# Decode attention with its key and value loads regrouped into four units of 32 KB rows, and its feed-forward part moved to the front

## The chip, the cores and the metric

The kernel runs on one core of a Trainium2 chip. The metric is the time of one execution in microseconds on the device. Executions of the same kernel differ, so each is called fast or slow: slow is a run more than 1.5 % above the fastest of the same kernel. The profile gives the span of the profiled execution, first to last instruction. The time is about 1.8 us longer than the span.

## The reference

Batch 2, one new token, 16 query heads on 8 key/value heads of size 256, a window of 2048 cached positions, and a small feed-forward part (FFN below) whose result gates the attention output.

```python
xn = layernorm(x)                                  # x: (2, 1, 448)
q  = xn @ wq                                       # 448 x 4096
s  = softmax(q @ K[window].T * 256**-0.5) @ V[window]
s  = s @ wo                                        # 4096 x 448
g  = silu(relu(xn @ w1) @ w2)                      # 448 x 1792, 1792 x 448
return x + s * g
```

K and V of the window are 33.6 MB of the 44.1 MB that the kernel reads. Each byte is used once, so the stream of loads is the floor: at the about 420 GB/s of the profile below, 44.1 MB take 105 us.

## The kernel before

K and V come as 16 transfers each of 1 MB, one per pair of head and batch, with 8 KB contiguous per partition. There are six K buffers and eight V buffers. One queue, that of the SP engine, issues all loads in order; a load waits until the buffer that it overwrites has been read.

```python
NT = W // 128; NKB = 6; NVB = 8
def kv_src(c, cache):                 # one head, one batch: 128 partitions x 8 KB
    hkv, b = divmod(c, 2)
    return cache[b, hkv, SK - W:SK, :].rearrange("(p t) d -> p (t d)", t=NT)
def load_k(c):
    d_k[c] = pr.dma(SP, kbuf[c % NKB][:, :], kv_src(c, A_k_cache), [last_T.get(c - NKB)])
def load_v(c):
    d_v[c] = pr.dma(SP, vbuf[c % NVB][:, :], kv_src(c, A_v_cache), [last_PV.get(c - NVB)])

load_k(0); load_k(1)
d_wq = pr.dma(SP, wqo[:, 0:SLOTS * HC], wq_src)
load_k(2); load_k(3)
# ... K and V alternate, V one pair behind K; and at the end of the program:
load_w1(0); load_w2(0)
# ... wo in five pieces, then on PE:
do_H(0); do_H(1); do_hT(); ...; do_F()          # the FFN
# ... 128 output matmuls with wo, gate, add x, store
```

PE transposes each K chunk (four 128x128 transposes, "T"), DVE or ACT copies the result from PSUM to SBUF (an eviction), PE multiplies by q (scores, "S"), softmax follows on DVE, PE and ACT, and PE multiplies the transposed weights by V ("PV").

Of the kernel before, what the change touches and what calls it, by code (L numbers as in the profile page):

```python
# [5 lines left out]
BF = mybir.dt.bfloat16  # L6
# [70 lines left out]
def bass_recurrent_scan__sliding_block_cached__dense_activation_relu__decode_kernel(  # L77
# [21 lines left out]
    NT = W // 128  # L99
    NPAIR = HKV  # L100
    NCH = 8
    SLOTS = 7
    NKB = 6
    NVB = 8
    NKT = 12
    NP = 3
    HC = HD // 2
    FC = DFF // 2
    WO_PARTS = [10, 10, 8, 2, 2]
    NCOL = D // 4  # L110

    es = contextlib.ExitStack()
    with es:
# [17 lines left out]
        qmask = named("qmask", [128, 4], F32)  # L131
        fold = named("fold", [128, 32], BF)
        gsum = named("gsum", [128, 128], F32)
# [8 lines left out]
        qz = named("qz", [128, 16 * NPAIR], BF)  # L142
# [7 lines left out]
        rm = [named(f"rm{i}", [128, 1], F32) for i in range(2)]  # L150
        mrow = [named(f"mrow{i}", [128, 128], F32) for i in range(2)]
        bias = [named(f"bias{i}", [128, 1], F32) for i in range(2)]
        e_sb = [named(f"e_sb{i}", [128, 512], BF) for i in range(2)]
        ssum = [named(f"ssum{i}", [128, 1], F32) for i in range(2)]
        rs = named("rs", [128, NPAIR], F32)
        pt = [named(f"pt{i}", [128, 64], BF) for i in range(NP)]
        o_sb = [named(f"o_sb{i}", [128, 512], BF) for i in range(2)]
        at_exp = named("at_exp", [128, 256], BF)
        at2 = named("at2", [128, 64], BF)
        wqo = named("wqo", [128, 32 * D], BF)  # L160
        assert SLOTS * HC <= 32 * D
        w1_sb = named("w1_sb", [128, SLOTS * FC], BF)
        w2_sb = named("w2_sb", [128, 14 * D], BF)
        kbuf = [named(f"kbuf{i}", [128, NT * DH], BF) for i in range(NKB)]
        vbuf = [named(f"vbuf{i}", [128, NT * DH], BF) for i in range(NVB)]
        kt = [named(f"kt{i}", [128, 1024], BF) for i in range(NKT)]

        tb = [psum(f"tb{i}", [128, 1024], BF) for i in range(3)]
        sbk = psum("sbk", [128, 512], F32)
        fbk = psum("fbk", [128, 512], F32)  # L170
        obk = [psum(f"obk{i}", [128, 512], F32) for i in range(2)]
# [6 lines left out]
        def kv_src(c, cache):  # L178
            hkv, b = divmod(c, 2)
            return cache[b, hkv, SK - W:SK, :].rearrange("(p t) d -> p (t d)", t=NT)  # L180

# [4 lines left out]
        d_k, d_v = {}, {}  # L186
        last_T, last_PV = {}, {}

        wq_src = A_wq.rearrange("r (hf c) -> (r hf) c", hf=2).rearrange("(p s) c -> p (s c)", s=SLOTS)
        w1_src = B_w1.rearrange("r (hf c) -> (r hf) c", hf=2).rearrange("(p s) c -> p (s c)", s=SLOTS)  # L190
        w2_src = B_w2.rearrange("(hf p j) n -> p hf (j n)", hf=2, j=7)
        wo_src = A_wo.rearrange("(p j) n -> p (j n)", j=32)

        def load_k(c):
            d_k[c] = pr.dma(SP, kbuf[c % NKB][:, :], kv_src(c, A_k_cache), [last_T.get(c - NKB)])

        def load_v(c):
            d_v[c] = pr.dma(SP, vbuf[c % NVB][:, :], kv_src(c, A_v_cache), [last_PV.get(c - NVB)])

        load_k(0)  # L200
        load_k(1)
        d_wq = pr.dma(SP, wqo[:, 0:SLOTS * HC], wq_src)
        load_k(2)
        load_k(3)
# [10 lines left out]
        p_mr = [pr.op(POOL, lambda e, t=t: e.memset(t[0:1, :], 0.0)) for t in mrow][-1]  # L215
        p_qz = pr.op(POOL, lambda e: e.memset(qz[:, :], 0.0), [p_one])

        a_z = [pr.op(ACTE, lambda e, t=t: e.memzero(t[:, :])) for t in (obk[0], sbk, obk[1], fbk)]  # L218
# [20 lines left out]
        def fold_op(e):  # L239
            with nc.allow_low_precision("zeros and ones"):  # L240
                return e.tensor_reduce(out=fold[:, :], in_=view(ident, 0, [[1, 32], [32, 4]]), axis=AX.X, op=ALU.add)
        v_fold = pr.op(DVE, fold_op)
        v_gs = pr.op(DVE, lambda e: e.tensor_copy(
            view(gsum, 0, [[32, 4], [1, 32]]), view(fold, 0, [[0, 4], [1, 32]])), [v_fold])
# [5 lines left out]
        for s in range(SLOTS):  # L250
# [4 lines left out]
            in1=view(par8, 0, [[1, SLOTS], [1, 2], [0, 2]]), op=ALU.mult), [m_xr, v_par8])  # L255

        evac, last_S, freed = {}, {}, set()
        st = {}

        def do_T(i):  # L260
            k, s = divmod(i, NCH)
            c = 2 * k + s // 4
            bank, src = tb[i % 3], kbuf[c % NKB]
            src_f, bank_f = src[:, :].bitcast(F32), bank[:, :].bitcast(F32)
            deps = [d_k[c], p_idf, evac.get(i - 3)]
            for n in range(4):
                lo = (4 * (s % 4) + n) * (DH // 2)
                o = pr.op(PE, lambda e, n=n, lo=lo: e.matmul(  # L268
                    bank_f[:, n * 128:(n + 1) * 128], lhsT=src_f[:, lo:lo + 128], rhs=ident_f[:, :],
                    start=True, stop=True, is_transpose=True), deps)  # L270
                deps = []
            last_T[c] = o
            if s % 4 == 3:
                freed.add((load_k, c))
            dst = kt[i % NKT]
            deps = [o, last_S.get(i - NKT)]
            if i % 2 == 0:
                evac[i] = pr.op(DVE, lambda e: e.tensor_copy(dst[:, :], bank[:, :]), deps)  # L278
            else:
                evac[i] = pr.op(ACTE, lambda e: e.activation(dst[:, :], bank[:, :], ACT.Copy), deps)  # L280

        def do_S(k, b):
            bank = sbk
            deps = [st["q"], a_z[1]] + ([st["exp", k - 1]] if b == 0 and k else [])
            for dhi in range(2):
                lhsT = qz[:, 16 * k + 8 * dhi + 4 * b:16 * k + 8 * dhi + 4 * b + 4]
                for i in range(4):
                    ch = NCH * k + 4 * b + i
                    o = pr.op(PE, mm(bank[32 * i:32 * i + 4, :], lhsT,
                                     view(kt[ch % NKT], dhi, [[2, 512]]),  # L290
                                     b == 0 and dhi == 0, b == 1 and dhi == 1, tile_position=(0, 32 * i)),
                              deps + [evac[ch]])
                    deps = []
            for i in range(4):
                last_S[NCH * k + 4 * b + i] = o
            st["S", k] = o

        def ch_max(k):
            st["rm", k] = pr.op(DVE, lambda e: e.tensor_reduce(  # L299
                out=rm[k % 2][:, :], in_=sbk[:, :], axis=AX.X, op=ALU.max),  # L300
                [st["S", k], st.get(("rmT", k - 2))])

        def ch_rmT(k):
            st["rmT", k] = pr.op(PE, lambda e: e.matmul(
                mbk_ap(0, 128, 1), lhsT=rm[k % 2][:, :], rhs=ident_f[:, :], start=True, stop=True,
                is_transpose=True), [st["rm", k], p_idf, st.get("mbk")])
            st["mrow", k] = st["mbk"] = pr.op(DVE, lambda e: e.tensor_reduce(
                out=view(mrow[k % 2], 0, [[32, 4], [1, 4]], n=1), in_=view(mbk, 0, [[0, 4], [1, 4], [32, 4]], n=1),
                axis=AX.X, op=ALU.max, negate=True), [st["rmT", k], p_mr, st.get(("bias", k - 2))])

        def ch_bias(k):
            st["bias", k] = pr.op(PE, mm(mbk_ap(128, 1), mrow[k % 2][0:1, :], one_f[0:1, :], True, True),
                                  [st["mrow", k], p_one, st["mbk"]])
            st["bsb", k] = st["mbk"] = pr.op(DVE, lambda e: e.tensor_copy(bias[k % 2][:, :], mbk_ap(128, 1)),  # L314
                                 [st["bias", k], st.get(("exp", k - 2))])

        def ch_exp(k):
            st["exp", k] = pr.op(ACTE, lambda e: e.activation(  # L318
                e_sb[k % 2][:, :], sbk[:, :], ACT.Exp, bias=bias[k % 2][:, 0:1],
                accum_out=ssum[k % 2][:, 0:1]), [st["bsb", k], st.get(("Pt", k - 2)), st.get(("gs", k - 2))])  # L320

        def ch_Pt(k):
            deps = [st["exp", k], st["mbk"]]
            for j in range(4):
                o = pr.op(PE, lambda e, j=j: e.matmul(  # L325
                    mb16[:, 512 + 128 * j:640 + 128 * j], lhsT=e_sb[k % 2][:, 128 * j:128 * j + 128],
                    rhs=ident[:, :], start=True, stop=True, is_transpose=True), deps)
                deps = []
            st["Pt", k] = o
            st["pt", k] = st["mbk"] = pr.op(DVE, lambda e: e.tensor_copy(  # L330
                view(pt[k % NP], 0, [[16, 4], [4, 4], [1, 4]]), view(mb16, 512, [[128, 4], [32, 4], [1, 4]])),
                [o, last_PV.get(2 * (k - NP) + 1)])

        def ch_sum(k):
            st["gs", k] = pr.op(PE, mm(mbk_ap(130, 1), gsum[:, :], ssum[k % 2][:, 0:1], True, True),
                                [st["mbk"], v_gs])
            st["rs", k] = st["mbk"] = pr.op(DVE, lambda e: e.reciprocal(rs[:, k:k + 1], mbk_ap(130, 1)), [st["gs", k]])

        def do_PV(k, s):
            b, j = divmod(s, 4)  # L340
            c = 2 * k + b
            bank, src, p = obk[k % 2], vbuf[c % NVB], pt[k % NP]
# [198 lines left out]
```

## Time and profile before

| | before, profile predicted from | before, a later fast profile |
|---|---|---|
| time (us), state | 117.39, slow | 114.55, fast |
| span (us) | 115.7 | 112.7 |
| last load of wo landed (us from the span's start) | 108.9 | 109.0 |
| from that byte to the end (us) | 6.8 | 3.8 |

The median time before was 115.65 us (three runs: 117.39, 114.65, 115.65).

First the slice table of the profile (40 equal slices of 2.9 us; digits are tenths, the last line is GB/s), then the chain of work that ended last, by engine.

```profile
PE   0009946980499799759989966999998695886390
PEclk9999999997559999985999998599999955555559
DMA  2998989999999999999999999999999999999200
GB/s 60 428 486 387 476 374 428 422 425 416 419 428 422 414 431 416 414 422 425 416 408 433 414 419 428 414 419 431 416 411 433 435 409 411 421 422 389 73 6 3
```

```profile
DMA 46%; PE 38%; DVE 6%; ACT 4%; issue 1%; POOL 1%; POOLq 0%
```

The loads run without a gap at about 420 GB/s from the second slice to the 37th. PE's clock falls to half now and then (0.5 in the records for 6.8 us from 27.3 us, for 3.4 us from 51.2 and from 71.7), and is at 0.5 from 92.2 to 112.7 us. The timeline of that end, on PE and SP (start, duration, what, and in brackets the idle time before it and its releaser):

```profile
98.15 2.77 PE L247 MATMUL fbk<-w_sb,xr 128*4 128x448 bf16 x7
101.63 2.77 PE L247 MATMUL fbk<-w_sb,xr 128*4 128x448 bf16 x7 [0.71 <-DVE h_n L404]
106.21 1.48 PE L247 MATMUL fbk<-w_sb,h_sb 128*2 128x112 bf16 x56
109.51 3.16 PE L247 MATMUL fbk<-wqo,at 128*2 128x112 bf16 x128 [1.81 <-DVE g_sb L428]
113.33 0.64 SPq L36 DMA_DIRECT2D out_dram<-out_sb  x1
```

In this execution the FFN's result g comes only after the last byte of wo is there (108.9): the output matmuls wait for it (`DVE g_sb`) until 109.51, and all 128 follow. The same lines of the later fast profile read differently:

```profile
96.63 2.77 PE L247 MATMUL fbk<-w_sb,xr 128*4 128x448 bf16 x7
100.10 1.49 PE L247 MATMUL fbk<-w_sb,xr 128*4 128x448 bf16 x7 [0.70 <-DVE h_n L404]
106.03 2.98 PE L247 MATMUL fbk<-wqo,at 128*2 128x112 bf16 x119 [1.82 <-DVE g_sb L428]
109.40 0.44 PE L247 MATMUL fbk<-wqo,at 128*2 128x112 bf16 x9 [0.38 <-issue]
110.49 0.63 SPq L36 DMA_DIRECT2D out_dram<-out_sb  x1
```

Here the FFN is done early, 119 of the 128 output matmuls run while wo still arrives, and the end hangs on the last byte. Its chain is 72 % DMA.

### The profile page before, as it was taken

The numbers are of one execution on the slowest core, as the hardware profiler recorded it, in microseconds if no ns is written. First come the engines' busy times: TensorE is split into PE (matmuls) and PEld (weight loads), VectorE is DVE, ScalarE is ACT, GpSimd is POOL, SyncE is SP. The second block draws the span as 40 slices with busy tenths as digits, with TensorE's granted clock in tenths as the row PEclk, the third lists the DMA queues.
The fourth block names the chain that finished last, engine by engine and source line by source line (L and its number), as shares of the span: only waits on it lengthen the run. The fifth ranks groups of instructions, "written<-read, shape, count | busy, mean of one in ns | idle before, by whom it ended". The sixth has DMA issues, their size and how long they took to land.

```text
span 115.7 us, 2285 instructions
## 1 busy us (share of the span) xinstructions
PE 85.0 (73%) x990; PEld 53.7 (46%) x990; DVE 49.4 (43%) x131; ACT 44.4 (38%) x57; POOL 1.9 (2%) x13
## 2 busy tenths in 40 slices
PE   0009946980499799759989966999998695886390
PEld 0009923650275465428556544756665342225280
DVE  2046424560027456523745742565575524113401
ACT  1951650668024834813384380348465010000000
POOL 6000000000000000000000000000000000000000
PEclk9999999997559999985999998599999955555559
DMA  2998989999999999999999999999999999999200
GB/s 60 428 486 387 476 374 428 422 425 416 419 428 422 414 431 416 414 422 425 416 408 433 414 419 428 414 419 431 416 411 433 435 409 411 421 422 389 73 6 3
DMA packets 5934, 44.26 MB, mean 383 GB/s; under 512 B 674, under 2 KB 932, under 8 KB 1316
## 3 DMA queue, kind: packets, MB, share of 16 engines
q1 hardware_dynamic: 5896, 44.11, 91.7%
q8 instruction: 8, 0.13, 0.5%
q14 instruction: 2, 0.02, 0.0%
q10 hardware_dynamic: 28, 0.00, 0.0%
HBM read 44.11 MB, written 0.00 MB: 381 GB/s over the span
## 4 chain that ended last, share of the span: by engine, by line
DMA 46%; PE 38%; DVE 6%; ACT 4%; issue 1%; POOL 1%; POOLq 0%
DMA kbuf<-in_A_k_cache_dram 46%; PE tb L268 13%; PE fbk L247 10%; PE obk L247 6%; PE sbk L247 3%; PE mbk L247 3%; PE mbk L325 2%; ACT L224 1%; ACT L218 1%; DVE xg L227 1%; DVE h_n L404 1%; ACT obk L218 1%; DVE o_sb L355 1%; DVE tmp L427 1%; DVE rm L299 1%
## 5 line engine op out<-in xcount | busy, mean ns | idle before, releaser
L268 PE MATMUL tb<-ident_f,kbuf 128*128 128x128 f32 x256 | 43.7, 307 | 9.8 <-DMA kbuf<-in_A_k_cache_dram 9.8
L280 ACT ACTIVATE kt<-tb 128x1024 bf16<-128x1024 bf16 x32 | 32.6, 1023 | 42.7 <-PE tb L268 42.7
L268 PEld LDWEIGHTS tb<-ident_f,kbuf 128*128 128x128 f32 x256 | 31.8, 158 | 17.5 <-DMA kbuf<-in_A_k_cache_dram 10.9
L278 DVE COPY kt<-tb 128x1024 bf16<-128x1024 bf16 x32 | 22.1, 689 | 23.6 <-PE tb L268 23.6
L247 PE MATMUL obk<-vbuf,pt 128*4 128x256 bf16 x256 | 13.7, 305 | 0.0
L247 PE MATMUL sbk<-kt,qz 128*4 128x512 bf16 x128 | 10.6, 410 | 0.1
L355 DVE TENSOR_SCALAR o_sb<-obk,rs 128x256 bf16<-128x256 f32 x16 | 7.5, 471 | 1.6 <-PE obk L247 1.6
L299 DVE TENSOR_REDUCE rm<-sbk 128x1 f32<-128x512 f32 x8 | 5.5, 692 | 6.0 <-PE sbk L247 6.0
L247 PEld LDWEIGHTS obk<-vbuf,pt 128*4 128x4 bf16 x256 | 4.5, 87 | 5.7 <-issue 3.5
L318 ACT ACTIVATE e_sb<-sbk,bias 128x512 bf16<-128x512 f32 x8 | 5.5, 683 | 3.7 <-DVE bias L314 3.7
L247 PE MATMUL mbk<-ident,xg 2*128 2x2 bf16 x7 | 0.3, 163 | 8.9 <-DVE xg L227 8.9
L247 PE MATMUL fbk<-w_sb,xr 128*4 128x448 bf16 x14 | 5.5, 573 | 0.7 <-DVE h_n L404 0.7
L424 ACT ACTIVATE ea<-fbk 128x112 f32<-128x112 f32 x1 | 0.3, 264 | 14.7 <-PE fbk L247 14.7
L247 PE MATMUL fbk<-wqo,at 128*2 128x112 bf16 x128 | 3.2, 298 | 1.8 <-DVE g_sb L428 1.8
L247 PEld LDWEIGHTS mbk<-ident,xg 2*128 2x128 bf16 x7 | 0.3, 101 | 8.9 <-DVE xg L227 8.9
L330 DVE COPY pt<-mbk 128x64 bf16<-128x64 bf16 x8 | 1.5, 192 | 6.4 <-PE mbk L325 6.4
L325 PE MATMUL mbk<-ident,e_sb 128*128 128x128 bf16 x32 | 4.0, 264 | 0.0
L247 PEld LDWEIGHTS mbk<-ssum,gsum 128*128 128x128 f32 x16 | 3.3, 258 | 1.2 <-DVE pt L330 1.0
L247 PEld LDWEIGHTS fbk<-wqo,at 128*2 128x2 bf16 x128 | 2.9, 124 | 2.1 <-DVE g_sb L428 2.1
L247 PE MATMUL mbk<-ssum,gsum 128*128 128x1 f32 x16 | 3.4, 281 | 0.6 <-DVE pt L330 0.6
L325 PEld LDWEIGHTS mbk<-ident,e_sb 128*128 128x128 bf16 x32 | 2.3, 114 | 2.8 <-DVE kt L278 1.3
L404 DVE TENSOR_SCALAR h_n<-fbk 4x448 bf16<-4x448 f32 x2 | 1.2, 612 | 5.4 <-PE fbk L247 5.4
(65 smaller groups left out, 48.7 us busy)
## 6 DMA issues: line engine op xcount, KB each, us to landing
kbuf<-in_A_k_cache_dram SPq DMA_DIRECT2D x16, 1024.0 KB, 24.5
vbuf<-in_A_v_cache_dram SPq DMA_DIRECT2D x16, 1024.0 KB, 25.5
wqo<-in_A_wq_dram SPq DMA_DIRECT2D x1, 3584.0 KB, 15.0
w_sb<-in_B_w_dram SPq DMA_DIRECT2D x2, 1568.0 KB, 25.9
wqo<-in_A_wo_dram SPq DMA_DIRECT2D x2, 1120.0 KB, 28.4
wqo<-in_A_wo_dram SPq DMA_DIRECT2D x1, 896.0 KB, 27.6
wqo<-in_A_wo_dram SPq DMA_DIRECT2D x2, 224.0 KB, 25.2
x_c<-in_A_x_dram ACTq DMA_DIRECT2D x2, 0.9 KB
```

Of the source, the lines that this page charges most:

```text
L218: a_z = [pr.op(ACTE, lambda e, t=t: e.memzero(t[:, :])) for t in (obk[0], sbk, obk[1], fbk)]
L224: a_sd = pr.op(ACTE, lambda e: e.activation(sd[0:B, 1:2], sd[0:B, 0:1], ACT.Sqrt), [v_ve])
L247: return lambda e: e.matmul(out_ap, lhsT=lhsT, rhs=rhs, start=start, stop=stop, skip_group_check=True, **kw)
L268: o = pr.op(PE, lambda e, n=n, lo=lo: e.matmul(bank_f[:, n * 128:(n + 1) * 128], lhsT=src_f[:, lo:lo + 128], rhs=ident_f[:, :], start=True ...
L278: evac[i] = pr.op(DVE, lambda e: e.tensor_copy(dst[:, :], bank[:, :]), deps)
L280: evac[i] = pr.op(ACTE, lambda e: e.activation(dst[:, :], bank[:, :], ACT.Copy), deps)
L299: st["rm", k] = pr.op(DVE, lambda e: e.tensor_reduce(out=rm[k % 2][:, :], in_=sbk[:, :], axis=AX.X, op=ALU.max), [st["S", k], st.get(("rmT ...
L318: st["exp", k] = pr.op(ACTE, lambda e: e.activation(e_sb[k % 2][:, :], sbk[:, :], ACT.Exp, bias=bias[k % 2][:, 0:1], accum_out=ssum[k % 2] ...
L325: o = pr.op(PE, lambda e, j=j: e.matmul(mb16[:, 512 + 128 * j:640 + 128 * j], lhsT=e_sb[k % 2][:, 128 * j:128 * j + 128], rhs=ident[:, :], ...
L330: st["pt", k] = st["mbk"] = pr.op(DVE, lambda e: e.tensor_copy(view(pt[k % NP], 0, [[16, 4], [4, 4], [1, 4]]), view(mb16, 512, [[128, 4], ...
L355: st["osb", k] = pr.op(DVE, lambda e: e.tensor_scalar(out=o_sb[k % 2][:, cols], in0=obk[k % 2][:, cols], scalar1=rs[:, k:k + 1], scalar2=N ...
L404: st["h_n"] = pr.op(DVE, lambda e: e.tensor_scalar(out=h_n[0:4, u * (FC // 2):(u + 1) * (FC // 2)], in0=fbk[0:4, 0:FC // 2], scalar1=0.0, ...
```

## The change

The intent: longer rows (32 KB per partition) for the loads; and no FFN in the tail, with its weights loaded at the front through the buffers that K and V need only later. The price is that there are only two K and two V buffers, of 32 KB per partition each.

```diff
-    NT = W // 128
-    NKB = 6
-    NVB = 8
+    NU = 4                     # units: 4 heads x 1 batch, 4 MB of K and of V
+    NT = 64
+    UW = NT * DH               # 32 KB per partition
+        kbuf = [named(f"kbuf{i}", [128, UW], BF) for i in range(2)]
+        vbuf = [named(f"vbuf{i}", [128, UW], BF) for i in range(2)]
+        wq_sb, w1_sb, w2_sb, wo_sb = vbuf[1], vbuf[0], vbuf[0], kbuf[0]
+        def load_k(u):
+            d_k[u] = pr.dma(SP, kbuf[u % 2][:, :], kv_src(u, A_k_cache), [st.get(("T", u - 2))])
+        def load_v(u, cuts=(0, NT)):
+            deps = [st["F_mm"] if u == 0 else st["q_mm"] if u == 1 else st["PV", u - 2]]
+            # ... one transfer for each cut
+        # queue: wq, K0, w1, w2, K1, then as below
+        do_q()
+        scores(0)
+        load_k(2)
+        softmax(0, [lambda: do_H(0), lambda: do_H(1), do_hT, do_F])
+        load_v(0)
+        scores(1)
+        load_k(3)
+        softmax(1, [lambda n=n: scores(2, n, n + 3) for n in (0, 3, 6, 9)])
+        load_v(1)
+        scores(2, 12)
+        softmax(2, [lambda g=g: do_PV(0, g) for g in ((0, 1), (2,), (3,))])
+        attend(0)
+        load_v(2)
+        scores(3)
+        softmax(3, [lambda: do_PV(1), lambda: attend(1)])
+        load_v(3, (0, 48, 64))
+        load_wo()
+        for u in (2, 3):
+            do_PV(u)
+            attend(u)
         # ... output matmuls
```

(Cut: scores use four heads at once and other heads are masked out; five PSUM banks for transposes instead of three; per unit nine evictions go to DVE and seven to ACT.) `scores(u)` is T and S of a unit; the list given to `softmax` is PE work placed into its waiting points. The order of this text is PE's order.

## The prediction

> **What bounds the kernel now.** The loads. The slice table holds 410 to 430 GB/s (44.26 MB in all) from slice 2 to slice 36[...]. PE is busy 73% and waits for K in gaps of 2 to 5 us (the waits: 9.8 us over 5). The stream never stops: loads are issued 25 us ahead. Then a tail: the timeline shows the FFN on PE from 98.2 to 109.2 us at granted clock 0.5, then 3.2 us of output matmuls, 0.6 us of DVE and 2.4 us for the store, ending at 115.7.
>
> **What the change removes.** (1) Row cost: 8 KB packets take a median of 312 ns, the 28 KB packets of wq 1062 ns. A line through both gives about 12 ns plus 0.0366 ns per byte, so a 32 KB row takes about 1.21 us; K and V (1,024 rows over 16 engines) take 77.6 us instead of 80.6. Gain 3 us. (2) The tail: with the FFN in front, the output matmuls follow the pieces of wo, and the end is the last byte plus about 3.7 us. Without any hole the kernel would end near 109.
>
> **What it adds.** Only two K and two V buffers of 4 MB remain, and a load waits for a whole unit's work. V3 waits for PV1, which PE, in order, reaches only after units 0 to 2 and T3; wo stands behind V3 on the same queue. PE's order, costed with the trace: a chunk (four transposes) 0.43 us at full clock[...]; eight score or PV matmuls 0.55; evictions 0.69 (DVE) and 1.02 (ACT), 9 and 7 per unit. Weights and K0 land near 11 and 21 us. Then, at full clock: T0/S0 to 33; softmax 0 with the FFN to 44; T1/S1 to 54; T2 woven into softmax 1 to 71 (PE often waits there for DVE); softmax 2, PV0 and attend to 78; T3/S3 to 89; PV1 to 91. The DMA would like V3 issued by about 85 (V2 lands near 86.5[...]). So 6 us of hole even then, giving 115.
>
> **The clock.** The trace drops to 0.5 for 3.4 us or more after PE was mostly idle (near 28, 52 and 72 us). The sparse softmax phases should cause this before T1, in T2 and before T3: about 2 us each, plus slower FFN. [...]transposes alone from 9.2 us had it at 1.0 by 14.05. So I expect recovery within each transpose block, and V3 starting nearer 96 than 92.7.
>
> **On the critical path.** Gains of 3 and about 3.5 us, against holes of roughly 0 to 1 us (K3), 0 to 3 us (V2) and 6 to 10 us (V3).
>
> **Predicted: 119.0 us, 80% range 113.0 to 124.5.** Faster by over 2%: 0.17; within 2%: 0.25; slower: 0.58.
>
> **What would show it.** Packets of 32 KB near 1.21 us; DMA slices at full until about 86 us, then a hole of 6 to 10 us before V3, its releaser PV1 on PE; F done by 48 us; half clock in the softmax phases; the chain running through PE, then V3 and wo.
>
> **What would make it wrong.** PE keeping full clock through the softmaxes, or the interleaved T2 hiding softmax 1 better than I counted: the V3 hole shrinks under 3 us and the kernel wins.

The sum behind 119.0: the span of 115.7, less 3 (rows) and about 3.5 us (tail), is about 109; the holes for K3, V2 and V3, 6 to 14 us in all, are added, and 119.0 leaves about 9.8 us for them. Two terms: a cost of the transposes at half clock, and a time from issue to first byte, which led from V2's landing near 86.5 to "by about 85". The profile doesn't show them as I had them: four transposes at half clock take 0.85 us (213 ns from one to the next), and from the start of the first load's issue to its first packet it is 1.1 us (0.74 to 1.80). The 119.0 is the figure with these terms in it.

## The result

| | before | changed |
|---|---|---|
| median time (us), all runs | 116.2 (114.65 to 117.39) | 121.63 (120.7 to 122.79) |
| ratio of fast runs | | 1.0574, 95 % interval 1.0499 to 1.0649 |
| the same two kernels again, later | 115.76 | 121.88; ratio 1.0623 (1.0499 to 1.0746) |

A ratio is the mean time of one kernel's fast runs over that of the other's of the same rounds, so it is not quite the ratio of the medians. The change made the kernel slower by 6 %. I had predicted slower, 119.0 us, or 2.9 % above 115.65. The time is inside the range; the change that I forecast is about half of the measured one.

The first profile of the changed kernel fell in a slow run (span 120.9), so the lines below are those of the repeat, a fast run with a span of 120.2 us. First the slices (3.0 us each) and the chain by engine.

```profile
PE   0010910799975299998464988479998529485470
PEclk9999997569999967999999999855999975555555
DMA  5999989999998989898999999999800299899920
GB/s 153 410 439 394 491 382 403 438 407 518 398 447 371 502 371 496 363 491 382 425 420 447 425 447 425 393 403 431 382 33 0 82 442 390 382 446 415 398 73 1
```

```profile
PE 46%; DMA 33%; DVE 11%; SPq 3%; ACT 3%; issue 2%
```

Three slices near 90 us carry almost nothing: 33, 0 and 82 GB/s. Against the profile before, the chain has moved from DMA to PE. What the queue waited for (total us, times, longest us):

```profile
SPq L36 <- PE tb L285: 39.7, 2, 29.2
SPq L36 <- PE mbk L323: 18.3, 1, 18.3
```

The first line is K2 and K3 waiting for transposes; the stream still had work in hand then. The second is the wait of V3. L323 is the small matmul for the maximum of softmax 3, in program order just behind PV1; the wait itself is on PV1, and the profile names the neighbour. It starts when V2 has been issued, so only its last part, after V2 has landed, costs anything. The timeline around it, PE and SP:

```profile
79.16 5.68 PE L285 MATMUL tb<-ident_f,kbuf 128*128 128x128 f32 x28
91.93 2.12 PE L265 MATMUL obk<-vbuf,pt 128*16 128x512 bf16 x32
94.08 1.18 SPq L36 DMA_DIRECT2D vbuf<-in_A_v_cache_dram  x2
95.31 2.68 SPq L36 DMA_DIRECT2D kbuf<-in_A_wo_dram  x5
114.62 2.01 PE L265 MATMUL obk<-kbuf,at 128*2 128x112 bf16 x72 [1.65 <-DMA kbuf<-in_A_wo_dram]
116.84 0.36 PE L265 MATMUL obk<-kbuf,at 128*2 128x112 bf16 x8 [0.21 <-DMA kbuf<-in_A_wo_dram]
117.86 0.66 SPq L36 DMA_DIRECT2D out_dram<-out_sb  x1
```

T3 begins at 79.16 with 28 transposes at half clock; PV1 (the 32 matmuls at 91.93) comes after all of T3/S3 and ends near 94; V3 is issued at 94.08. V2's last packet had ended at 88.87 (its completion signal came at 89.3), and V3's first packet starts at 95.41: 6.5 us with nothing in flight. The last load of wo lands at 116.8, and the end follows 3.4 us later.

To see the loads as a ledger, I took the bytes that the packet records put into each microsecond and counted what is missing against 430 GB/s (my reference; the steady part of the changed kernel shows 433), in microseconds of lost load time. Packets and instructions are counted from one zero, the first instruction; in an earlier count my packet times were about half a microsecond late. A load has landed when its completion signal came, 0.4 to 0.5 us after its last packet in these profiles.

```
profile of             24-74 us   74-84   84-100   wo landed   span
before, slow             1.2       0.2      0.4      108.9     115.7
before, fast             1.2       0.2      0.3      109.0     112.7
changed, fast            0.4       0.5      8.6      116.8     120.2
```

The hole costs 8.6 us, the rows give back about 0.8 us in the steady part, and the last byte is 7.8 us later. From the last byte to the end the changed kernel needs 3.4 us. The kernel before needs 3.8 us in its fast profile, so the whole difference of 7.5 us in span is the late last byte, less 0.4 us.

### The profile page after: what moved, and what is told of

It is laid out like the page before. It is cut to its first block, busy times and chain, and to the rows that moved or that the text cites. A ratio compares the mean times of both kernels' runs of the same rounds, so it can differ in the third digit from the quotient of the medians.

```text
span 120.9 us, 1849 instructions
## 1 busy us (share of the span) xinstructions
PE 77.3 (64%) x810; PEld 50.9 (42%) x810; DVE 48.6 (40%) x111; ACT 35.5 (29%) x42; POOL 1.9 (2%) x11
## 4 chain that ended last, share of the span: by engine, by line
PE 46%; DMA 33%; DVE 11%; SPq 3%; ACT 3%; issue 2%
PE tb L285 30%; DMA kbuf<-in_A_k_cache_dram 17%; DMA kbuf<-in_A_wo_dram 16%; PE sbk L265 8%; PE obk L265 5%; DVE kt L293 3%; SPq L36 3%; DVE s_sb L335 2%; PE mbk L265 2%; ACT e_sb L340 2%; DVE rm L318 2%; DVE h_n L418 1%; PE mbk L345 1%; PE mbk L323 1%; ACT kt L295 1%
## 5 line engine op out<-in xcount | busy, mean ns | idle before, releaser
L285 PE MATMUL tb<-ident_f,kbuf 128*128 128x128 f32 x256 | 39.4, 316 | 5.1 <-DMA kbuf<-in_A_k_cache_dram 5.1
L295 ACT ACTIVATE kt<-tb 128x1024 bf16<-128x1024 bf16 x28 | 27.8, 1022 | 41.0 <-PE tb L285 41.0
L285 PEld LDWEIGHTS tb<-ident_f,kbuf 128*128 128x128 f32 x256 | 35.0, 166 | 11.2 <-issue 5.8
L293 DVE COPY kt<-tb 128x1024 bf16<-128x1024 bf16 x36 | 24.9, 691 | 26.4 <-PE tb L285 26.3
L265 PE MATMUL sbk<-kt,qz 128*32 128x512 bf16 x128 | 12.0, 394 | 2.0 <-DVE kt L293 1.5
L265 PE MATMUL obk<-vbuf,pt 128*16 128x512 bf16 x128 | 11.5, 493 | 1.1 <-DMA vbuf<-in_A_v_cache_dram 1.1
L265 PE MATMUL obk<-vbuf,xr 128*4 128x512 bf16 (+1 forms) x42 | 6.1, 534 | 4.0 <-DMA vbuf<-in_A_wq_dram 4.0
L265 PEld LDWEIGHTS obk<-vbuf,pt 128*16 128x16 bf16 x128 | 3.6, 105 | 6.1 <-issue 2.8
L373 DVE TENSOR_SCALAR o_sb<-obk,rs 128x512 bf16<-128x512 f32 x4 | 3.0, 740 | 7.6 <-PE obk L265 7.6
L265 PE MATMUL obk<-kbuf,at 128*2 128x112 bf16 x128 | 3.3, 270 | 2.8 <-DMA kbuf<-in_A_wo_dram 2.8
L323 PE MATMUL mbk<-ident_f,rm 128*1 128x128 f32 x4 | 1.1, 270 | 3.8 <-DVE rm L321 3.8
```

Of the source, the lines that this page charges most:

```text
L265: return lambda e: e.matmul(out_ap, lhsT=lhsT, rhs=rhs, start=start, stop=stop, skip_group_check=True, **kw)
L285: o = pr.op(PE, lambda e, n=n, lo=lo: e.matmul(bank_f[:, n * 128:(n + 1) * 128], lhsT=src_f[:, lo:lo + 128], rhs=ident_f[:, :], start=True ...
L293: evac[n_th] = pr.op(DVE, lambda e: e.tensor_copy(dst[:, :], bank[:, :]), deps)
L295: evac[n_th] = pr.op(ACTE, lambda e: e.activation(dst[:, :], bank[:, :], ACT.Copy), deps)
L323: m = st["rmT", u] = pr.op(PE, lambda e: e.matmul(mbk_ap(0, 128, 1), lhsT=rm[:, :], rhs=ident_f[:, :], start=True, stop=True, is_transpose ...
L373: ob = st["obk"] = pr.op(DVE, lambda e: e.tensor_scalar(out=o_sb[:, :], in0=obk[:, :], scalar1=rs[:, u:u + 1], scalar2=None, op0=ALU.mult) ...
```

## The experiments

My theory: V3's load stands behind PV1, PV1 stands behind T3/S3 in PE's order, and half clock in and after the sparse softmax phases delays both (mean granted clock 0.88 from 72 to 79 us and 0.80 from 79 to 92 in the repeat of the changed kernel). Rivals: the queue order alone (wo could fill the hole) explains the loss; or PE's chain after the hole is as long as the loads, so that closing the hole changes little; and, for the missing gains, that rows and tail were worth less than I thought.

### The two kernels again

Two runs of unchanged kernels, for more profiles.

> The kernel before, unchanged, for a profile in the fast state: the profile that I predicted from was of the slowest of its runs. The first experiment on it (FFN in front, 112.8 us span, ratio 0.998) says that the FFN in the tail costs nothing in a fast run. If that is so, this profile has the full clock in the tail, the FFN done before the last wo pieces land, and the end about 3.5 us after the last wo byte, with a span near 112.5. If the span is 112.5 for another reason (a faster load stream), the last wo byte lands well before 108.5.

Measured: 115.68 us, span 113.9, a single run of unknown state, and not what I expected: again with the FFN at half clock (two blocks of 2.77 us from 96.44 and 99.92).

> The changed kernel, unchanged, on the same chip as the next two and for a profile in the fast state: ratio 1.05 to 1.06, span near 119.5, the hole before V3 about 8 us, V3 issued near 95 after PV1.

Measured: 121.88 us, ratio 1.0623; profile above.

### PV1 ahead of T3

```diff
         attend(0)
         load_v(2)
-        scores(3)
-        softmax(3, [lambda: do_PV(1), lambda: attend(1)])
+        do_PV(1)
         load_v(3, (0, 48, 64))
         load_wo()
+        scores(3, 0, 3)
+        attend(1)
+        scores(3, 3)
+        softmax(3)
```

> One part undone: PV1 (and attend 1) run before T3 instead of after it, so V3 may be issued at about 82 us instead of 95. Order theory (V3 waits for PV1 behind T3): the 8 us hole in the load stream is gone, V3 plus wo take about 18.5 us instead of 20.9, the last byte lands near 108 and the span is 110 to 112 us (ratio to before about 0.97). Clock theory (half clock is what makes the chain late): only a part of the hole goes, span 115 or more. Row theory (32 KB rows or the 4 MB head steps load slowly): slices stay at the present rate and the span stays above 117.

Measured: 120.67 us median (118.46 to 120.84; three of four runs slow, so no ratio). The hole is gone: 0.2 us lost between 84 and 100 us instead of 8.6, last byte at 109.2 instead of 116.8. That part of the theory stands. But the one fast run's span is still 116.7 us (fast runs of the changed kernel: 118.9 to 121.3), a miss of what I expected. The profile is of a slow run, of span 119.0; its timeline of PE at the end suggests why, and a fast run shows the same end below (PV1 and PV2 early):

```profile
102.13 3.59 PE L265 MATMUL obk<-vbuf,pt 128*16 128x512 bf16 x32
106.79 3.59 PE L265 MATMUL obk<-vbuf,pt 128*16 128x512 bf16 x32
112.83 3.16 PE L265 MATMUL obk<-kbuf,at 128*2 128x112 bf16 x128 [0.29 <-DVE at L492]
```

PV2, PV3 and the output matmuls wait for no load any more. They run one after the other at half clock (0.50 in the records from 98 to 113 us; 3.59 us for the 32 matmuls that take 2.12 at 91.93 above), behind T3 and softmax 3. Behind the hole stood a second limit, PE's own chain, nearly as late.

### wo in front of V3

```diff
         load_v(2)
+        load_wo()
         scores(3)
         softmax(3, [lambda: do_PV(1), lambda: attend(1)])
         load_v(3, (0, 48, 64))
-        load_wo()
```

> Only the order of two loads: wo is issued before V3, no compute moved. Order theory: wo fills the hole (wo lands near 97), V3 is issued at 95 as now and lands near 107, and then PV3, attend and all 128 output matmuls follow it, about 9 us: span near 117 (4 us less than the changed kernel, still slower than or equal to before). If the hole is not a matter of what is in the queue, the stream still has an empty stretch after V2 and the span stays at 120.

Measured: 120.05 us, ratio 1.0358 (1.0196 to 1.052); spans of the two fast runs 116.5 and 117.7. The profile is of a slow run. In it wo fills the hole (it has landed by 98.7 us); V3 is the last load, in two pieces that land at 107.0 and 109.5. PV3 stands idle for the first piece and starts as it lands:

```profile
107.05 3.59 PE L265 MATMUL obk<-vbuf,pt 128*16 128x512 bf16 x32 [2.49 <-DMA vbuf<-in_A_v_cache_dram]
```

PV3, attend and all output matmuls (from 113.09) then follow at half clock (0.50 from 98 to 113 us), as expected. So here the end hangs on the late V3 and on PE's work behind it. The queue order is a cause of the hole's cost, as the rival says, but mending it gains 2 % of the 6 %, by two fast runs.

### PE kept busy in softmax 0 and 2

Transposes of the identity into free banks, with no use but to keep PE busy; order and loads as in the changed kernel.

```diff
+        def spin(n):
+            for i in range(n):
+                # transpose of ident_f into tb[i % NTB], no waits
-        softmax(0, [lambda: do_H(0), lambda: do_H(1), do_hT, do_F])
+        softmax(0, [also(lambda: do_H(0), 12), also(lambda: do_H(1), 4), also(do_hT, 10), do_F])
-        softmax(2, [lambda g=g: do_PV(0, g) for g in ((0, 1), (2,), (3,))])
+        softmax(2, [also(lambda: do_PV(0, (0, 1)), 3), lambda: do_PV(0, (2,)),
+                    also(lambda: do_PV(0, (3,)), 9), lambda: spin(3)])
+        spin(7)
```

> Changed kernel plus idle-time transposes into free PSUM banks during softmax 0 and softmax 2 (12, 4, 10 and 3, 9, 3, 7 of them). Clock theory: T1 and T3 run at full clock from their start, V3 is issued about 4 us earlier (near 91) and the span falls by about 4 us; the hole shrinks from 8 to 4 us. Order theory alone: at most the same 4 us and never more, a hole of at least 4 us remains. If the clock does not matter for the end: span unchanged at 120.

Measured: 118.06 us (117.98 to 118.4), ratio 1.0285 (1.0202 to 1.0369), 3.6 to 3.8 us less than the changed kernel's two medians and as expected. The clock line of the slices, and the start of T3 and the issue of V3 in the timeline:

```profile
PEclk9999999999999999999999999999999975555555
```

```profile
77.52 3.26 PE L285 MATMUL tb<-ident_f,kbuf 128*128 128x128 f32 x28
90.05 1.18 SPq L36 DMA_DIRECT2D vbuf<-in_A_v_cache_dram  x2
```

The 28 transposes at the start of T3 take 3.26 us instead of 5.68 (those of T1 3.40 instead of 4.68), V3 goes out 4.0 us earlier, and the loads lost at the hole fall from 8.6 to 4.8 us. So the clock is a cause by itself, worth nearly 4 us, and about half of the hole remains.

### PV1 and PV2 early, without and with the busy PE

The first of these makes PE's order follow the loads better: PV1 after four chunks of T3, PV2 inside softmax 3. The second adds the idle transposes, in softmax 3 too.

```diff
-        scores(3)
-        softmax(3, [lambda: do_PV(1), lambda: attend(1)])
+        scores(3, 0, 4)
+        do_PV(1)
         load_v(3, (0, 48, 64))
         load_wo()
-        for u in (2, 3):
-            do_PV(u)
-            attend(u)
+        scores(3, 4, 7)
+        attend(1)
+        scores(3, 7)
+        softmax(3, [lambda: do_PV(2), lambda: attend(2)])      # second: + spin(9), spin(4)
+        do_PV(3)
+        attend(3)
```

> As the first experiment, PV1 moved ahead of most of T3, and also PV2 moved into the wait of softmax 3, nothing kept warm. Theory after the first batch: with the hole gone the end is set by PE's own chain after T3, at half clock (softmax 3, PV2 3.6, PV3 3.6, output matmuls 3.2 us). PV2 inside softmax 3 takes about 4 us off that chain: span near 114, load stream still ending near 107 to 109. If instead the load stream sets the end, the span stays where the first experiment had it (116.7 in its fast run).

Measured: 116.39 us, ratio 1.0142 (1.0032 to 1.0252), span 115.6 in the profile, of a fast run. The loads end at 109.7 us, and PE, at half clock again (0.50 from 104 to 109 us), is the end:

```profile
103.41 3.59 PE L265 MATMUL obk<-vbuf,pt 128*16 128x512 bf16 x32
109.44 3.09 PE L265 MATMUL obk<-kbuf,at 128*2 128x112 bf16 x128 [0.29 <-DVE at L492]
```

> The same with the idle-time transposes in all of softmax 0, 2 and 3, so that T1, T3 and the last PVs run at full clock. Theory: PE's chain shortens by another 4 us or more and falls below the load stream, so the end is last byte (near 107) plus 3.5: span 110.5 to 111.5, ratio to before 0.975 to 0.99, the first version that beats both. If PE's chain still sets the end, the span is 112 to 114 and the out matmuls start after wo has landed.

Measured: 112.91 us (112.51 to 114.44), ratio 0.9809 (0.9689 to 0.9929), span 110.7. Repeated:

> The best version again (V3 not behind T3, PV2 in softmax 3, PE kept warm), with five rounds and beside the next: ratio to before 0.975 to 0.985, span near 110.8, last wo byte near 107.4.

Measured: 113.27 us, ratio 0.9899 (0.9845 to 0.9953), a smaller gain than I expected. It beats both kernels, the one before by 1 to 2 %, which is not clearly more than 2 %. Clock and loads in the slices of the first of these runs, and its end on PE:

```profile
PEclk9999999999999999999999999999999999999955
DMA  6799999999999999999999999999899899999930
```

```profile
98.43 1.90 PE L265 MATMUL obk<-vbuf,pt 128*16 128x512 bf16 x32
105.13 2.00 PE L265 MATMUL obk<-kbuf,at 128*2 128x112 bf16 x72 [1.65 <-DMA kbuf<-in_A_wo_dram]
107.34 0.36 PE L265 MATMUL obk<-kbuf,at 128*2 128x112 bf16 x8 [0.20 <-DMA kbuf<-in_A_wo_dram]
```

No hole is left (0.1 us lost between 84 and 100 us), PV3 takes 1.90 us, and the output matmuls wait for wo: the end is the last byte, 107.3, plus 3.4 us. This is the version in which the loads alone set the end. Order and clock together explain the loss: the mean time of fast runs goes from 122.1 (changed) to 116.6 (order) to 112.8 (order and clock), 9.4 us.

### The same with 8 KB rows

The same kernel as the last, each unit loaded as four transfers of 8 KB rows; what waits for what is unchanged.

```diff
+        Q = [(lo, lo + NT // 4) for lo in range(0, NT, NT // 4)]
-            d_k[u] = pr.dma(SP, kbuf[u % 2][:, :], kv_src(u, A_k_cache), [...])
+            d_k[u] = [pr.dma(SP, kbuf[u % 2][:, lo * DH:hi * DH],
+                             kv_src(u, A_k_cache)[:, :, lo * DH:hi * DH], [...]) for lo, hi in Q]
```

> The best version with one thing undone: each K or V unit is loaded as four transfers of 8 KB rows instead of one of 32 KB rows; every wait is still for the whole unit. Row theory as predicted (8 KB 312 ns, 32 KB 1.21 us): 3 us longer stream, span 113.8. As measured since (means 315 and 1223 to 1226 ns, with the slow packets at each restart): 1.5 to 2.3 us, span 112.3 to 113. If the row length does not matter and only the order does: span as its neighbour, 110.8.

Measured: 114.5 us, ratio to the kernel before 1.001 (0.9979 to 1.0041). The mean of its fast runs is 114.43 us, that of the version with 32 KB rows 113.17. So the long rows are worth 1.3 us, not the 3.0 of my sum. The difference is below the 1.5 to 2.3 us that I expected from the means, though the span, 112.5, is within its range. One stretch of 10 us in the steady part shows a part of the reason. After the stretch and its length come the busy us, with the number of instructions, of PE, PE's weight loads, DVE, ACT and POOL; the last three columns are PE clock, mean busy DMA engines as a share of 16, and GB/s. First the 8 KB version, then the changed kernel.

```profile
59.00:69.00 10.00, 7.38 (x71) 5.24 (x72) 5.16 (x11) 5.42 (x8) 0.00 (x0) 1.00 1.01 422
```

```profile
66.00:76.00 10.00, 8.59 (x93) 4.79 (x91) 5.68 (x13) 3.12 (x4) 0.00 (x0) 1.00 1.00 433
```

With 8 KB rows the packet records add up to more than 16 engines (1.01): neighbouring packets overlap in the records. My 80.6 us was packets times their duration, so the overlap, about 1 us, was in it. From the rates instead, 33.55 MB take 79.5 us at 422 and 77.5 us at 433 GB/s, 2.0 us. The packets of 32 KB have the median that I predicted (1214 ns), but a mean of 1226, with some up to 2.1 us; in the stretch shown their mean is 1215. The 11 ns between these means, over 64 packets on each engine, are 0.7 us: an estimate from these numbers, which leaves the 1.3 us measured.

### The kernel before with the FFN at the front

The other gain by itself: w1 and w2 behind wq, the FFN after q, all else as before.

```diff
         d_wq = pr.dma(SP, wqo[:, 0:SLOTS * HC], wq_src)
+        st["w1"] = pr.dma(SP, w1_sb[:, :], w1_src)
+        st["w2"] = pr.dma(SP, w2_sb[...], w2_src)
-        load_w1(0); load_w2(0); ... do_H(0); do_H(1); do_hT(); do_F()      # at the end
+        for fn in (lambda: do_H(0), lambda: do_H(1), do_hT, do_F):
+            at_step(NCH - 1, 1, fn)                                          # after q
```

> The kernel before with one part of the change alone: w1 and w2 loaded behind wq and the FFN done right after q; 1 MB loads, buffers and all else as before. If the FFN in the tail cost what I read from the timeline (last wo byte at 108.9, end at 115.7, of which 3.4 us are needed), the span falls by about 3 us (ratio 0.97). If the early loads of w1 and w2 starve the K transposes later, it falls by less or not at all.

Measured: 114.55 us (114.36 to 115.04), ratio 0.9981 (0.9896 to 1.0065): nothing gained over fast runs, where I expected about 3 us. Its four runs were all fast, while three of seven runs of the kernel before took 115.9 us or more. That agrees with its tail no longer depending on PE's clock, but four runs are few. To compare fast runs alone also drops those executions of the kernel before whose tail was the longest; over all runs, slow ones too, the means are 115.37 and 114.63 us, a gain of 0.7 us, still far from 3.

### The kernel before with PE kept busy in its tail

```diff
+        for i in range(NCH * NPAIR + 4, max(steps) + 1):
+            at_step(i, 6, lambda: spin(2))
         do_H(0)
+        spin(5)
         do_H(1)
+        spin(5)
         do_hT()
+        spin(4)
         ...
         do_F()
+        spin(12)
```

> The kernel before, nothing moved, with idle-time transposes into free PSUM banks in the last softmax, the last PVs and between the FFN's matmuls. Theory: the FFN in the tail costs time only when the clock there is half (first profile: end 6.8 us after the last wo byte; second 4.9); at full clock it is finished before wo has landed. Then every run ends about 3.5 us after the last wo byte, span 112.3 to 113, no run over 115 in time, as with the FFN in front. If the FFN itself costs the tail whatever the clock, the spans stay spread over 112.5 to 116.

Measured: 115.12 us (114.72 to 116.26), ratio 1.0092 (1.0031 to 1.0152), a miss. The FFN blocks did take 1.49 us instead of 2.77, but the filler itself delayed the start of the FFN to 101.0 us. The slowest of the six runs was 116.3 us against 118.7 of the kernel before. So it doesn't settle what fast and slow runs of that kernel differ in.

### More profiles of the kernel before

Three runs of the unchanged kernel, in search of the profile of a fast execution.

> The kernel before once more, unchanged, for a profile of one of its fast runs (span 112.2 to 112.9, clock 0.90 to 0.93 in the records), of which there is none yet; ratio to itself 1. If my tail gain of 3.5 us was read from a slow run only: the last wo byte lands near 109 as in both earlier profiles, but the two FFN blocks of seven matmuls take 1.5 us each instead of 2.77, the output matmuls wait for wo and not for g, and the end comes 3.3 to 3.9 us after the last byte. If instead a fast run is fast through an earlier stream, the last wo byte lands near 106.

Measured: 116.06 us median; the profiled run was slow (span 115.0), with both FFN blocks at 2.77 us, from 97.55.

> The kernel before, for a profile of a fast run. Tail theory: last wo byte near 109 in this one too; if it is a fast run (span 112.2 to 112.9) the FFN ends earlier (its matmul blocks at 1.5 us instead of 2.77, or started earlier) and the output matmuls wait for wo; end 3.3 to 3.9 us after the last byte. If it is a slow run, end 5 to 7 us after it, as three times before.

Measured: a profile of a fast run, 114.55 us, span 112.7. The first FFN block takes 2.77 us, the second 1.49.

> As the one before it: a second chance for a profile of a fast run; the same numbers.

Measured: slow again in the profile, span 115.4, FFN blocks 2.77 us from 97.94 and 101.42.

In all five profiles of the kernel before, fast and slow, the last byte of wo lands between 108.9 and 109.0 us. What differs is the clock in the FFN, and when the FFN starts; together they decide whether it hides under the last loads or ends the kernel. The clock in the stretches 94:98, 98:104, 104:109 and 109:113, first in the profile that I predicted from, then in the fast one (the columns are as above):

```profile
94.00:98.00 4.00, 2.76 (x38) 1.44 (x38) 1.78 (x7) 0.00 (x0) 0.00 (x0) 0.50 0.99 402
98.00:104.00 6.00, 5.29 (x16) 1.58 (x16) 0.79 (x2) 0.00 (x0) 0.00 (x0) 0.50 1.01 421
104.00:109.00 5.00, 2.69 (x67) 1.87 (x65) 2.08 (x6) 0.26 (x1) 0.00 (x0) 0.50 0.70 277
109.00:113.00 4.00, 3.16 (x128) 2.89 (x128) 0.69 (x3) 0.00 (x0) 0.00 (x0) 0.54 0.02 4
```

```profile
94.00:98.00 4.00, 2.81 (x28) 1.11 (x25) 1.32 (x4) 0.00 (x0) 0.00 (x0) 0.50 1.00 412
98.00:104.00 6.00, 4.30 (x74) 2.05 (x74) 1.74 (x5) 0.00 (x0) 0.00 (x0) 0.87 1.01 420
104.00:109.00 5.00, 3.09 (x139) 2.40 (x124) 1.35 (x3) 0.26 (x1) 0.00 (x0) 0.74 0.68 271
109.00:113.00 4.00, 0.46 (x12) 0.17 (x8) 0.55 (x2) 0.00 (x0) 0.00 (x0) 0.90 0.01 3
```

The three slow profiles each have a stretch of 3.41 us at half clock that begins between 69.8 and 71.7 us, and their FFN starts at 97.55 to 98.15. The two others (112.7 and 113.9 us) have none between 56 and 92 us, and start it at 96.63 and 96.44. This is the fast profile's clock line, to be held against the one in the section on the profile before (slices 25 and 26):

```profile
PEclk9999999999558999996799999999999995589859
```

So half clock in the FFN at an early start (113.9 us) accounts for 1.2 us of the 3.0 between 112.7 and 115.7; the rest goes with the late start. No run tested the two apart.

## Why the prediction was right or wrong

The direction and the cause were right, and the size was wrong. By point:

- **V3 behind PV1, wo behind V3: right.** I predicted a hole of 6 to 10 us there. The trace has 6.5 us with no packet in flight and 8.6 us of lost load time. F was done by 43.3 us (predicted: by 48). K3 and V2 made no hole worth naming (0.4 us lost between 24 and 74 us, 0.5 between 74 and 84).
- **PE's stages: right within 2 us up to the last.** Predicted ends at full clock: T0/S0 33, softmax 0 44, T1/S1 54, T2 71, PV0 78, T3/S3 89. Seen at about 34.5, 44, 56, 72, 79 and 92, the last with half clock at its start. V3's first byte, predicted "nearer 96 than 92.7", came at 95.4.
- **The clock: right.** Half clock at the start of T1 and T3 cost about 4 us by the run with PE kept busy. T2 was not affected (clock 1.00 from 55 to 72 us in the repeat): woven with softmax 1, PE was busy for 12.0 of the 17 us; there I was too cautious. Under transposes alone PE came to full clock, as I had read from the trace: the kernel before does nothing but transposes on PE from 9.2 us until wq has landed at 16.7, and its first clock record, near 13.7 us, is to 1.0 (my 14.05 was a little late): before it the transposes start 213 ns apart, after it 109 ns. And idle transposes in two softmax phases raised the mean clock of the changed kernel from 0.836 to 0.907 in the same order. That the clock fell after PE was "mostly idle" was put too strongly: in the 3.41 us before the drops at 27.3, 51.2 and 71.7 us PE was busy for 52, 42 and 46 %.
- **The step that failed: "Gains of 3 and about 3.5 us".** The terms of the sum:

| term (us) | predicted | measured | by |
|---|---|---|---|
| long rows | -3.0 | -1.3 | 8 KB rows in the version without a hole |
| FFN out of the tail | -3.5 | -0.2 (-1.2 to +0.7) | the kernel before with the FFN at the front; interval of its ratio times the mean of before |
| order and clock | +9.8 (what 119.0 leaves for it) | +9.4 | changed kernel against early PV1 and PV2 with busy PE, fast means |
| sum | +3.3 | +7.9 | |

Measured directly, the fast means of the repeat are 122.1 and 115.0 us, a difference of 7.2; the 0.7 us between that and the sum is within what two calls differ by (the version without a hole was 2.2 us faster than before in one and 1.2 us in the other).

The tail was mis-sized because I read it from one profile, of a run of 117.39 us, the slowest of the three that I had. In the fast profile the FFN hides under the loads, and there is nothing for the front position to give. The rows were mis-sized because I multiplied packets by their durations, which overlap, and took the median for the mean.

A second slip hid this in the absolute number. My sum started from a span, 115.7 us, and gave a span, 119.0. Fast spans of the changed kernel in the repeat are 119.8 to 121.3 us, so as a span it was about 1 us low. But I set it against the median time, 115.65 us, which happened to be the same number. A span of 119.0 would have been a time of 120.8, by the 1.8 us between the two. The base was 3 us too high for a fast span (115.7 against 112.7), and the tail gain of 3.5 us, real only for such a slow run, cancelled it. That the absolute number missed by no more than 2.6 us was luck; the change, +3.3 us forecast against 7.2 measured, was under half.

- **What I had not seen.** Even without the hole the changed order is not fast: PE's chain of T3, softmax 3, PV2, PV3 and the output matmuls, at half clock, ends at almost the same time. With the hole removed alone, the three fast runs have spans of 116.5 to 117.7 us (changed kernel: 118.9 to 121.3); keeping the clock up alone gained 3.6 to 3.8 us in median time, and both with PV2 moved forward 9.4 us.

Left open: why the clock of the kernel before comes back in the FFN in some executions and not in others. The granted clock changes in steps of 3.41 us in the records (in the first profiles of the two kernels every stretch between two changes is a multiple of it, 3.41 to 30.72 us), and an FFN block at half clock lasts 2.77 us, so where a block falls in such a step may decide it. The five profiles agree with it: the one block after which the clock rose (96.63 to 99.40, fast profile) lies whole inside one step (96.11 to 99.52, counted on from the recorded changes), and each of the eight blocks of the other four crosses the end of a step. But another step, with PE busy for 92 % of it (92.18 to 95.60 in the first profile, not yet FFN), didn't bring the clock back, and no run tested it. Also open are a dip of the loads near 76 to 79 us, where some packets of the changed kernel take much longer, and whether the best version is more than 1 % faster than before.

## What to carry to other kernels

When few large buffers replace many small ones behind an in-order queue, ask for each load which instruction must end before it can be issued, and where that instruction stands in its engine's order; here one PV behind a whole unit of transposes cost 8.6 us of loads. Size a gain from the profile of a fast run, compare spans with spans, and check that the profiled run is like the median run before its tail is read as typical. A limit removed may expose another just behind it, so try the mends together before judging either.

## What the traces show of clock and loads

- Clock and transposes: fp32 transposes of 128x128 alone were all that PE did from 9.2 us to the first record of 1.0 at 13.7 us in the kernel before. Put into the softmax phases of the changed kernel, beside its few matmuls there, they kept the clock from falling (1.00 from 24 to 55 and from 72 to 92 us), and the 28 transposes at the start of T3 took 3.26 us instead of 5.68.
- Clock and busy PE: only 1.0 and 0.5 occur in the clock records of the first profiles of the two kernels. To be busy was not enough for the full clock: in the kernel before, FFN matmuls kept PE busy for 5.29 of 6.00 us (98 to 104 us) and the clock stayed at 0.50.
- Rate of the loads in a steady stretch of 10 us: 433 GB/s with rows of 32 KB (changed kernel, repeat), 422 with rows of 8 KB. A row of 8 KB took 312 ns (median) and one of 32 KB 1214 ns, and the change from one to the other was worth 1.3 us in 33.6 MB.
- Restart of the loads: from the start of the issuing instruction of V3 to its first packet, with no load in flight, it was 1.3 us (94.08 to 95.41), of which the instruction itself is 0.5. The three microseconds from that packet's start carried 169, 354 and 422 GB/s (in the first profile of the changed kernel 145, 326 and 421, where the first eight packets of V3 took 1.71 to 1.95 us against a median of 0.91).
